# Attention and a mixture of experts on one core: the router steps' maximum moved, a second xT buffer, and late splits, one-hots and transposes placed later

## The chip, the cores and the metric

The kernel runs on one core of one Trainium2 chip. A core has a matrix engine (TensorE, PE in the profile; its weight loads are listed as PEld), a vector engine (VectorE, DVE), an activation engine (ScalarE, ACT), a general engine (GpSimd, POOL) and a queue that issues transfers (SyncE, SP). The engines run their own streams of instructions in order and wait for each other by semaphores. The metric is the device time of one execution in microseconds; lower is better.

## The reference

Attention over 8 batches, 8 heads, 576 positions and head size 64, with two masks: the first four heads see the last 32 positions ("local"), the other four see the positions with the same remainder modulo 32 ("strided"). The result, 4608 tokens of 512 numbers, goes through a mixture of 8 experts, each token through one of them at most.

```python
mask_local = (rel >= 0) & (rel < 32)
mask_strided = (rel >= 0) & (pos[None, :] % 32 == pos[:, None] % 32)
scores = np.where(masks[None], scale * q @ k.T, -1e9)      # heads 0-3 local, 4-7 strided
attn = exp(scores - max(scores)); attn /= attn.sum() + 1e-9
x = (attn @ v).transpose(0, 2, 1, 3).reshape(4608, 512)
skip_score = x @ w_skip; logits = x @ w_gate
e_idx = argmax(logits); gate_w = softmax(logits)[e_idx]
for e in range(8):
    h = maximum(x[mask_e] @ w1[e], 0)
    y[mask_e] = gate_w * (h @ w2[e])
out = x + y where skip_score > 0, else x
```

## The kernel before

Attention is cut into 32 units, four per batch: the local heads' blocks in two halves, `pr` 0 (blocks 0 to 4) and 1 (blocks 5 to 8), and the strided heads' in two halves, `pr` 2 and 3. The main loop (line 879) runs one step `n` for each unit and keeps a software pipeline: in step n it computes the scores of unit n+2 (`qk`), the exponentials of unit n (`tex`: transposes on PE, exponentials on ACT), the product with v of unit n-1 (`pv`) and the transposes of the output of unit n-2 (`xpose`, into the tile `xT`). All four are generators: each `next` issues one stage, so the loop writes the order of the engines' streams by hand.

`qk` has three stages: the score matmuls into the single PSUM buffer S (L211); the addition of the mask on DVE (L219 local, L221 strided), which frees S; the maximum on DVE (L225) with its subtraction on POOL (L227). `pv` has two: the matmuls into the single buffer PV (L281), and the normalization on DVE (L290, L291, L297), which frees PV. `tex` of the unit waits for POOL's subtraction (transposes at L247, exponentials at L255).

Each batch also has router work. `score` (L342; copied to `s64` by ACT at L349 and L351) multiplies the transposed outputs `xT` with the router's weights, at step `pr` 2 of the next batch; in that step the new batch's local outputs are transposed ahead of it on PE, and ACT copies them into `xT` (L327). At `pr` 3, the "router step", `route1` transposes the scores (L366) and makes the decision in a chain of ten small DVE operations (L371 to L389); one step on `route2` ranks the tokens (matmuls L416 to L422, DVE L429 to L433). Some steps later `gates` (L406 to L410) splits the gate values, `hot` makes one-hot tiles on DVE (`heh` L451, `hlo` L454), `mul` makes `hpm` on POOL (L462), and `place` (L470) multiplies them on PE into a table of tokens for each expert; the dictionary `plan` gives the step of each for each batch. At step 29 the table of batches 0 to 5 is finished (`tabled`, L481 to L486), and POOL gathers the rows of the first expert, key "e" (L639). Its weights come early: `FETCH` gives the steps at which their loads are issued on SP (L586, three buffers `raw`), `CASTS` those at which ACT makes the high part (L597), `RESTS` those at which DVE makes the low part (`wrest`, L603), which frees the raw buffer.

Router steps differ by batch. Up to batch 5 (`CB`) the router's DVE chain comes last in the step, and the maximum of that step's `qk` (the local second half of the next batch, 768 wide) is held (`held`) until the next step, behind that step's mask. From batch 6 on the whole router decision is run ahead of `tex` and of the mask.

On PE, DVE and POOL the order is that of the program; ACT and SP are ordered by the compiler's planner within the dependencies. After the loop (L995) PE transposes the gathered rows (`xrows`, L675, with the split of the result at L678 and L679), the expert's first product starts (`ffn1a`, L721), and the seven other experts follow, each as three matmuls for the split operands (L682 to L684).

Of the kernel before, what the change touches and what calls it, by code (L numbers as in the profile page):

```python
# [9 lines left out]
F32 = mybir.dt.float32  # L10
F32R = mybir.dt.float32r
BF16 = mybir.dt.bfloat16
# [7 lines left out]
B, H, S, D = 8, 8, 576, 64  # L20
# [6 lines left out]
SQ = 3 * NA  # L27
SB = 11
# [15 lines left out]
PB = 3  # L44
CB = 5
CASTS = [(6, 0), (6, 2)]
RESTS = [(6, 3), (7, 0)]
FETCH = [(6, 0), (6, 1), (6, 2), (7, 1)]
CE = (96, 3)

# [56 lines left out]
def attn_moe(ctx: ExitStack, tc: tile.TileContext, q, k, v, w9d, w1d, w2d, cst, out, NB=B):  # L107
# [22 lines left out]
    psum, bufs = pctx.enter_context(tc.tile_pool(name="psum", bufs=1, space=PSUM)), {"S": 1, "T": 4, "PV": 1}  # L130

    def ps(tag, n=1):
        return psum.tile([128, n, 512] if n > 1 else [128, 512], F32, name=tag, tag=tag, bufs=bufs[tag])
# [3 lines left out]
    ap = actx.enter_context(tc.tile_pool(name="apool", bufs=1))  # L137
# [26 lines left out]
    def passed(m):  # L164
        mark[:] = [m.ins]
# [14 lines left out]
    def loadq(b, kind):  # L180
        t, d = qtile(b, kind)
        for j in range(2):
            paced(t[:, j], d[:, j])
# [129 lines left out]
    xT_ = {}  # L313

    def xpose(b, pr):
        kind, b0, b1 = UNITS[pr]
        if b0 == 0:
            xT_[b, kind] = ap.tile([128, 2, (S, SB * SQ)[kind]], F32, name=f"xT{kind}", tag=f"xT{kind}", bufs=1)
        x, nq = xt_[b, kind], (HP, SQ)[kind]
        for g in range(b0, b1, 4):  # L320
            m = min(4, b1 - g)
            t = ps("T")
            for y in range(m):
                i = T.transpose(t[:, y * 128:(y + 1) * 128], x[:, g + y, :], ident)  # L324
            passed(i)
            yield
            A.copy(xT_[b, kind][:, :, g * nq:(g + m) * nq].rearrange("p i (n q) -> p n i q", q=nq),  # L327
                   t[:, 0:m * 128].rearrange("p (n i q) -> p n i q", i=2, q=HP)[:, :, :, 0:nq])
# [4 lines left out]
    def tiles(g):  # L333
        return GT
# [108 lines left out]
    def hot(g):  # L443
        o = slice(GOFF[g], GOFF[g + 1])

        def sp(n, shape, dt=F32, bufs=1):
            return ap.tile([128, GT] + shape, dt, name=n, tag=n, bufs=bufs)

        q, c = hot_[g]
        eh = sp("heh", [24], BF16)  # L450
        V.tensor_tensor(eh, con["eh"].unsqueeze(1).broadcast_to([128, GT, 24]),  # L451
                        c.unsqueeze(2).broadcast_to([128, GT, 24]), op=ALU.is_equal)
        lo = sp("hlo", [128], BF16, 2)
        V.tensor_tensor(lo, con["iom"].unsqueeze(1).broadcast_to([128, GT, 128]),  # L454
                        q.unsqueeze(2).broadcast_to([128, GT, 128]), op=ALU.is_equal)
        hot_[g] = lo, eh
# [364 lines left out]
    def weave(a, b):  # L821
        def chain(gs):
            for g in gs:
                yield from g
        a, b = chain(a), chain(b)
        live = [a, b]
        while live:
            for g in list(live):
                if next(g, 0) == 0:
                    live.remove(g)  # L830
# [9 lines left out]
    def run(*gs):  # L840
        weave(gs, [])
# [27 lines left out]
    mark.clear()  # L869
    fill = setup()  # L870
    tvw = table.rearrange("(e r) c -> e r c", e=NE)
    late, ranked, held = [], None, []

    plan = {x: (4 * x + 8, 4 * x + 10, 4 * x + 10, 4 * x + 12) for x in range(CB - 1)}
    plan[CB - 1] = (4 * CB + 4, 4 * CB + 5, 4 * CB + 5, 4 * CB + 7)
    plan[CB] = (4 * CB + 7, 4 * CB + 7, 4 * CB + 7, 4 * CB + 9)
    pool_order = ExitStack()
    pool_order.enter_context(tc.manual_schedule(engines={G.engine, T.engine, V.engine}))
    for n, (b, pr) in enumerate(units):

        ahead = n // 2 + 3
        qk_, v_, out_ = pr % 2 and ahead // 2 < NB, pr % 2 == 0 and b + 1 < NB, n > 3 and units[n - 4 + (pr + 1) % 2]
        if n == 8:
            spare = tvw[:, CMAX:CE[0] * CE[1] + CT, :].rearrange("e (a n) c -> a e (n c)", n=NE)
            nc.sync.dma_start(spare, fill.rearrange("p n c -> p (n c)")[0:spare.shape[0]].unsqueeze(1)
                              .broadcast_to([spare.shape[0], NE, 4 * NE]))
        if n + LA >= len(units) and "h" not in pool:
            zctx.close()
            pool["h"] = ctx.enter_context(tc.tile_pool(name="hpool", bufs=1, side="right", reuse_waits="tile"))
        g = [i for i, x in enumerate(GROUPS) if x[1] == b]  # L890

        front = [qk(*units[n + LA])] if n + LA < len(units) else []
        if n > 0:
            front.append(pv(*units[n - 1]))
        seq = [tex(b, pr)]
        if g and pr == 2:
            seq = [xpose(*units[n - 2])] + seq
        for x in front[:-1]:
            next(x)

        if late and b > CB:
            run(*late)
            late = []
            norm(g[0])
            ranked = g[0]
        if n > 0:
            run(seq.pop(0))
        if late:
            next(late[0])
        if qk_:  # L910
            loadq(ahead // 2, ahead % 2)
        if v_:
            loadv(b + 1, pr // 2, (0,))
        next(front[-1])
        if qk_:
            loadk(ahead // 2, ahead % 2)
        if v_:
            loadv(b + 1, pr // 2, (1,))
        put = [place(x) for x, it in plan.items() if it[3] == n]
        full = n == plan[CB][3]  # L920
        rank = []
        if ranked is not None:
            rank = [route2(ranked, of=COUNTED.get(b if pr else b - 1))]
            for _ in range(tiles(ranked) + 1):
                next(rank[0])
            ranked = None
        for x in front:
            next(x, 0)
            if held:
                run(*held)  # L930
                held = []
        if late:
            run(*rank, *late, *front[1:])
            held = front[:1]
        else:
            run(*rank, *front)
        if full:
            run(*put)
            tabled()
        late = []  # L940
        if b > 0 and pr == 2:
            seq = [score(b - 1)] + seq
        if n > 1 and not (g and pr == 2):
            seq.append(xpose(*units[n - 2]))
        run(*seq)
        if v_:
            loadv(b + 1, pr // 2, (2,))
        if out_:
            store(out_[0], out_[1] // 2, (pr % 2,))
        if not full:  # L950
            run(*put)
        if g and pr == 2:
            late = [route1(g[0])]
        if g and pr == 3 and b <= CB:
            norm(g[0])
            ranked = g[0]
        if b == PB + 2 and pr == 1:
            picked = pick(PB)
            next(picked)
        if b == PB + 2 and pr == 2:  # L960
            run(picked)
        if (b, pr) in RESTS:
            j = RESTS.index((b, pr))
            wrest("e", j, j + 1)
        if (b, pr) in CASTS:
            j = CASTS.index((b, pr))
            wcast("e", j, j + 1)
        if b == CB + 2 and pr == 3:
            count(CB)
        if n == 1:  # L970
            G.tensor_copy(parts[:, :, 0:2], con["pk"].rearrange("p (t c) -> p t c", c=2))
        for x, it in plan.items():
            for f, at in zip((gates, hot, mul), it):
                if at == n:
                    f(x)
        if b == PB + 2 and pr == 3:
            e0 = nc.sync.value_load(isel[0:1, 0:1], min_val=0, max_val=NE - 1)
            wdma("e", e0, 0, 1)
        if b == PB + 2 and pr == 3:
            s0 = G.value_load(isel[0:1, 0:1], min_val=0, max_val=NE - 1)  # L980
        if (b, pr) in FETCH:
            j = FETCH.index((b, pr)) + 1
            wdma("e", e0, j, j + 1)
        if b == CB + 2 and pr == 1:
            at, P = seat("e", *CE), CE[0]
            for c, dt in ((slice(0, 2), I32), (slice(2, 3), F32)):
                G.tensor_copy(at[:, :, c].bitcast(dt),
                              tabs[:P, bass.ds(s0, 1), 0:CE[1], c].rearrange("p o n c -> p (o n) c").bitcast(dt))
            gather("e", "e", "e", last=(CB + 1) * S)
# [16 lines left out]
    psum, bufs = pctx.enter_context(tc.tile_pool(name="psumT", bufs=1, space=PSUM, reuse_waits="tile")), {"S": 2, "T": 3, "PV": 2, "R": 1}  # L1006
# [24 lines left out]
    psum, bufs = ctx.enter_context(tc.tile_pool(name="psumB", bufs=1, space=PSUM, reuse_waits="tile")), {"S": 4, "T": 2, "PV": 2}  # L1031

    seq = [("e", e0, 6), ("e", e0, 7)]
# [176 lines left out]
```

## Time and profile before

| | |
|---|---|
| median of 3 runs | 441.22 us (441.03 to 444.55) |
| profiled execution | 442.9 us, its span 441.4 us |
| PE busy | 408.3 us (93%) |
| DVE busy | 274.9 us (62%) |
| ACT busy | 185.6 us (42%) |
| POOL busy | 144.8 us (33%) |
| mean granted clock of PE | 0.965 |
| moved by DMA | 90.39 MB |

The span runs from the first to the last instruction; the profiled execution's own time holds 1.5 us more around it. Attention takes the first 175 us, the experts the rest. A row of the timeline gives the start and the duration in us, the engine, the line, the operation, what it writes and reads, how often, and in brackets how long the engine was idle before it and what ended that. A row of the windows gives a stretch, its length, the busy time of PE, PEld, DVE, ACT and POOL with the number of instructions, the granted clock of PE, the DMA engines' busy share and GB/s. A row of the waits gives the waiting instruction, what released it, the total us, the count and the longest.

### The profile page before, as it was taken

The numbers are of one execution on the slowest core, as the hardware profiler recorded it, in microseconds if no ns is written. First come the engines' busy times: TensorE is split into PE (matmuls) and PEld (weight loads), VectorE is DVE, ScalarE is ACT, GpSimd is POOL, SyncE is SP. The second block draws the span as 40 slices with busy tenths as digits, with TensorE's granted clock in tenths as the row PEclk, the third lists the DMA queues.
The fourth block names the chain that finished last, engine by engine and source line by source line (L and its number), as shares of the span: only waits on it lengthen the run. The fifth ranks groups of instructions, "written<-read, shape, count | busy, mean of one in ns | idle before, by whom it ended". The sixth has DMA issues, their size and how long they took to land.

```text
span 441.4 us, 12232 instructions
## 1 busy us (share of the span) xinstructions
PE 408.3 (93%) x4991; PEld 367.1 (83%) x4992; DVE 274.9 (62%) x597; ACT 185.6 (42%) x361; POOL 144.8 (33%) x201
## 2 busy tenths in 40 slices
PE   5989899988988788998999999999999999999994
PEld 3867767767676668798898799999999999999984
DVE  3566879797997866760594564374564654855611
ACT  1345453644537244532642444453543544545400
POOL 3434445454644653214052236032023132201201
PEclk8899999999999685999999999999999999999998
DMA  8999999799989354535257467366475565645101
GB/s 294 398 343 293 307 317 320 249 331 304 311 250 351 107 157 110 168 98 138 97 190 211 130 215 225 127 192 196 140 235 154 191 198 184 212 148 189 47 21 43
DMA packets 51774, 90.39 MB, mean 205 GB/s; under 512 B 8091, under 2 KB 27931, under 8 KB 51713
## 3 DMA queue, kind: packets, MB, share of 16 engines
q1 hardware_dynamic: 45249, 79.19, 54.5%
q0 software_dynamic: 6464, 10.37, 8.2%
q8 instruction: 40, 0.66, 0.6%
q14 instruction: 21, 0.17, 0.1%
HBM read 75.16 MB, written 14.91 MB: 204 GB/s over the span
## 4 chain that ended last, share of the span: by engine, by line
PE 71%; DMA 9%; DVE 7%; ACT 6%; POOL 3%; issue 2%; SPq 1%; POOLq 0%; ACTq 0%; DVEq 0%
PE S L682 16%; PE S L684 16%; PE S L683 16%; PE PV L281 6%; DMA vt<-in_vp_dram 3%; PE T L324 3%; PE T L247 3%; PE S L211 3%; ACT s L351 2%; PE T L342 2%; PE PV L774 2%; DMA qt<-in_qp_dram 2%; DMA xg<-out_dram,tab 2%; PE T L661 1%; POOL sm L227 1%
## 5 line engine op out<-in xcount | busy, mean ns | idle before, releaser
L682 PE MATMUL S<-xh,w1h 128*128 128x342 f32 (+6 forms) x248 | 78.5, 316 | 0.0
L762 POOL DMA_INDIRECT out_dram<-ot,tab x25 | 28.0, 1119 | 152.7 <-DVE ot L760 142.9
L684 PE MATMUL S<-xh,w1l 128*128 128x342 f32 (+6 forms) x248 | 76.8, 310 | 0.0
L683 PE MATMUL S<-xl,w1h 128*128 128x342 f32 (+6 forms) x248 | 76.7, 309 | 0.0
L682 PE MATMUL S<-hh,w2h 128*128 128x288 f32 (+5 forms) x192 | 59.5, 310 | 0.7 <-DVE hl L695 0.7
L684 PE MATMUL S<-hh,w2l 128*128 128x288 f32 (+5 forms) x192 | 58.0, 302 | 0.0
L683 PE MATMUL S<-hl,w2h 128*128 128x288 f32 (+5 forms) x192 | 58.0, 302 | 0.0
L694 ACT ACTIVATE hh<-S 128x342 fp32r<-128x342 f32 (+6 forms) x64 | 27.9, 436 | 64.1 <-PE S L684 55.9
L603 DVE TENSOR_TENSOR w1l<-raw,w1h 128x1024 fp32r<-128x1024 f32 x32 | 39.0, 1223 | 18.6 <-ACT w1h L597 17.8
L682 PEld LDWEIGHTS S<-xh,w1h 128*128 128x128 f32 x248 | 46.9, 189 | 0.7 <-DVE hl L695 0.5
L683 PEld LDWEIGHTS S<-xl,w1h 128*128 128x128 f32 x248 | 46.8, 189 | 0.1
L684 PEld LDWEIGHTS S<-xh,w1l 128*128 128x128 f32 x248 | 46.7, 188 | 0.0
L603 DVE TENSOR_TENSOR w2l<-raw,w2h 128x1024 fp32r<-128x1024 f32 x32 | 39.1, 1223 | 9.8 <-ACT w2h L597 9.6
L327 ACT COPY xT<-T 128x512 f32<-128x512 f32 (+4 forms) x56 | 22.2, 441 | 53.6 <-PE T L324 30.1
L227 POOL TENSOR_TENSOR sm<-sm,mx 128x480 f32<-128x480 f32 (+1 forms) x32 | 32.2, 1026 | 37.9 <-DVE mx L225 26.6
L639 POOL DMA_INDIRECT xg<-out_dram,tab x25 | 33.1, 1323 | 32.7 <-issue 10.1
L695 DVE SCALAR_TENSOR_TENSOR hl<-S,hh 128x342 fp32r<-128x342 f32 (+6 forms) x64 | 30.9, 483 | 20.2 <-ACT hh L694 18.8
L211 PE MATMUL S<-kt,qt 64*64 64x54 f32 (+1 forms) x1280 | 32.7, 243 | 8.2 <-DMA kt<-in_kp_dram 3.3
L211 PEld LDWEIGHTS S<-kt,qt 64*64 64x64 f32 x1280 | 27.0, 142 | 14.5 <-DVE sm L219 3.5
L682 PEld LDWEIGHTS S<-hh,w2h 128*128 128x128 f32 x192 | 36.2, 188 | 1.0 <-DVE hl L695 1.0
L683 PEld LDWEIGHTS S<-hl,w2h 128*128 128x128 f32 x192 | 36.3, 189 | 0.0
L684 PEld LDWEIGHTS S<-hh,w2l 128*128 128x128 f32 x192 | 36.2, 189 | 0.0
(182 smaller groups left out, 792.9 us busy)
## 6 DMA issues: line engine op xcount, KB each, us to landing
raw<-in_w_dram SPq DMA_DIRECT2D x64, 512.0 KB
vt<-in_vp_dram SPq DMA_DIRECT2D x40, 390.0 KB
qt<-in_qp_dram SPq DMA_DIRECT2D x16, 304.0 KB
kt<-in_kp_dram SPq DMA_DIRECT2D x16, 297.0 KB
out_dram<-x SPq DMA_DIRECT2D x16, 288.0 KB
kt<-in_kp_dram SPq DMA_DIRECT2D x14, 304.0 KB
qt<-in_qp_dram SPq DMA_DIRECT2D x14, 288.0 KB
out_dram<-x SPq DMA_DIRECT2D x32, 99.0 KB
```

Of the source, the lines that this page charges most:

```text
L211: m = T.matmul(s[HP * (i ^ j):HP * (i ^ j) + HP, j, (blk - b0) * win:(blk - b0 + 1) * win], lhsT=qt[p, j, blk * nq:blk * nq + HP], rhs=kt[ ...
L227: G.tensor_tensor(e[:, j], e[:, j], mx[:, j].unsqueeze(2).broadcast_to([128, b1 - b0, win]), op=ALU.subtract)
L281: x = T.matmul(p[HP * i:HP * i + HP, bank, slot * 65:slot * 65 + 65], lhsT=pt[a:z, m, j, i ^ j, :], rhs=vt[a:z, (b0 if kind == 0 else b0 / ...
L327: A.copy(xT_[b, kind][:, :, g * nq:(g + m) * nq].rearrange("p i (n q) -> p n i q", q=nq), t[:, 0:m * 128].rearrange("p (n i q) -> p n i q" ...
L603: V.tensor_tensor(lo, raw_.pop((key, j)), hi.bitcast(F32), op=ALU.subtract)
L639: i = G.indirect_dma_start(out=xg[:s["P"], t, :], out_offset=None, in_=out[0:last, :], in_offset=bass.IndirectOffsetOnAxis(ap=s["tab"][:s[ ...
L682: T.matmul(p, lhsT=a[0], rhs=b[0], start=start, stop=False)
L683: T.matmul(p, lhsT=a[0], rhs=b[1], start=False, stop=False)
L684: T.matmul(p, lhsT=a[1], rhs=b[0], start=False, stop=stop)
L694: A.activation(s["hh"][:, f, :C], p[:, :C], AF.Relu)
L695: V.scalar_tensor_tensor(s["hl"][:, f, :C], p[:, :C], 0.0, s["hh"][:, f, :C].bitcast(F32), op0=ALU.max, op1=ALU.subtract)
L762: i = G.indirect_dma_start(out=out, in_=ot[:P], in_offset=None, bounds_check=NTOK - 1, oob_is_err=False, out_offset=bass.IndirectOffsetOnA ...
```

## The change

Five things move. The local `xT` has two buffers instead of one, the strided one still has one; `hlo` has one instead of two. At the router steps up to batch 5 the maximum (and POOL's subtraction) comes right behind its mask, ahead of the normalization and of the router's DVE chain; nothing is held. At batch 6's router step the mask comes first, then `tex`, then the router's decision with its transposes, then the normalization, the ranks and the maximum; at batch 7's, which has no `qk`, `tex` comes ahead of the router's decision. `hot` and `mul` of batch 5 come at step 28 instead of 27. The low parts of the first two weight tiles (`RESTS`) come at steps 29 and 30 instead of 27 and 28.

```diff
-RESTS = [(6, 3), (7, 0)]
+RESTS = [(7, 1), (7, 2)]
...
-            xT_[b, kind] = ap.tile([128, 2, (S, SB * SQ)[kind]], F32, name=f"xT{kind}", tag=f"xT{kind}", bufs=1)
+            xT_[b, kind] = ap.tile([128, 2, (S, SB * SQ)[kind]], F32, name=f"xT{kind}", tag=f"xT{kind}", bufs=2 - kind)
...
-        lo = sp("hlo", [128], BF16, 2)
+        lo = sp("hlo", [128], BF16)
...
-    late, ranked, held = [], None, []
+    late, ranked = [], None
...
-    plan[CB] = (4 * CB + 7, 4 * CB + 7, 4 * CB + 7, 4 * CB + 9)
+    plan[CB] = (4 * CB + 7, 4 * CB + 8, 4 * CB + 8, 4 * CB + 9)
...
+        masked = late and b > CB and len(front) > 1
+        if masked:
+            next(front[0])
+        if n > 0:
+            run(seq.pop(0))
         if late and b > CB:
             run(*late)
             late = []
             norm(g[0])
             ranked = g[0]
-        if n > 0:
-            run(seq.pop(0))
...
-        for x in front:
+        for x in front[1:] if masked else front:
             next(x, 0)
-            if held:
-                run(*held)
-                held = []
-        if late:
-            run(*rank, *late, *front[1:])
-            held = front[:1]
-        else:
-            run(*rank, *front)
+            if late:
+                run(x)
+        run(*rank, *late, *front)
```

## The prediction

> **What bounds the kernel now.** The page's busy times come first, then the waits of TensorE in the attention steps, then the busy times of one batch.
>
> ```profile
> PE 408.3 (93%) x4991; PEld 367.1 (83%) x4992; DVE 274.9 (62%) x597; ACT 185.6 (42%) x361; POOL 144.8 (33%) x201
> ```
> ```profile
> PE T L247 <- POOL sm L227: 4.5, 8, 0.8
> PE T L247 <- ACT s L351: 1.7, 5, 0.3
> ...
> PE T L366 <- ACT pts L255: 1.1, 5, 0.2
> ```
> ```profile
> 116.77:135.57 18.80, 16.87 (x414) 13.34 (x409) 17.72 (x50) 8.90 (x22) 11.66 (x18) 1.00 0.87 283
> 135.57:159.62 24.05, 18.62 (x359) 14.79 (x350) 18.70 (x52) 11.11 (x23) 12.16 (x20) 0.86 0.60 192
> ```
>
> TensorE (PE) is busy 93% of the span, so whatever ends its waits is gain. The waits table covers 38 to 130 us: 4.5 us on GpSimd's subtraction of the maximum, 1.7 + 1.1 us behind ScalarE's copies of the scores. The last two rows (PE, weight loads, DVE, ACT, POOL, clock, DMA share, GB/s) are one batch of steps each, about the 6th and the 7th: the later one takes 5.2 us more and shows a clock of 0.86. VectorE (DVE) is the next engine: 17.7 of 18.8 us.
>
> **Part 1, the maximum behind its mask, steps 7 to 23.** At these router steps the maximum of the local second half is held until the next step.
>
> ```profile
> 98.55 0.96 DVE L219 TENSOR_TENSOR sm<-S,cs 128x768 f32<-128x768 f32 x1
> 101.43 0.17 DVE L290 TENSOR_SCALAR rc<-PV 128x12 f32<-128x12 f32 x1 [1.92 <-PE PV L281]
> ...
> 105.63 0.94 DVE L225 TENSOR_REDUCE mx<-sm 128x8 f32<-128x768 f32 x1
> ...
> 120.23 0.17 DVE L290 TENSOR_SCALAR rc<-PV 128x12 f32<-128x12 f32 x1
> ...
> 129.52 0.17 DVE L290 TENSOR_SCALAR rc<-PV 128x10 f32<-128x10 f32 x1 [0.26 <-PE PV L281]
> ```
> ```profile
> 106.72 1.61 POOL L227 TENSOR_TENSOR sm<-sm,mx 128x384 f32<-128x384 f32 x2 [1.56 <-DVE rc L290]
> ...
> 128.53 1.42 POOL L227 TENSOR_TENSOR frame<-frame,mx 128x324 f32<-128x324 f32 x2 [1.40 <-DVE mx L225]
> ```
>
> The mask ends at 99.51 and DVE then sits idle for 1.92 us. The 0.94 us maximum fits there (99.51 + 0.94 = 100.45, before 101.43), and the subtraction ends about 5 us earlier, so the 4.5 us of waits go. Queued behind the inserted maximum are the normalization and the router's DVE chain; while the slot is idle nobody waits. It is not idle at the fifth such step: between 101.43 and 129.52 DVE never pauses, and at 120.23 its normalization started right after the mask, so there it comes 0.86 us later.
>
> **Part 2, two xT buffers.**
>
> ```profile
> 115.33 0.75 ACT L327 COPY xT<-T 128x512 f32<-128x512 f32 x2 [3.36 <-PE T L342]
> ```
>
> ACT stands idle 3.36 us until the score matmuls have read the single buffer, then copies for 0.75 us ahead of the score copies. With a second buffer the copy falls into the idle time, the score copies start some 0.7 us earlier, and the 0.34 + 0.22 us waits of L247 and L366 (1.7 + 1.1 over five batches) go.
>
> ```profile
> PE T L247 <- POOL sm L227: 2.1, 4, 0.8
> ```
>
> This row is the same wait from 38 to 100 us only. Sum of both parts up to step 26: 4 x 0.56 + 2.1 = 4.4 by 101 us. In the stretch where DVE never pauses 3.0 us of waits are removed, but DVE is relieved by one maximum (0.86) only; followed through its order, the gain of PE at 130 us is 1.7, the S buffer and the PV buffer being free in time. **Term 1: 6.1 us.** Bounds: 7.3 if DVE did not matter, 0 if transfers take over.
>
> **Part 3, steps 27 to 30.** Here the long stall of the trace lies.
>
> ```profile
> 136.93 0.50 PE L366 MATMUL T<-cs,s 41*128 41x41 f32 x5 [0.90 <-ACT s L351]
> ...
> 148.03 1.33 PE L211 MATMUL S<-kt,qt 64*64 64x54 f32 x40 [3.04 <-DVE frame L221]
> ...
> 151.17 2.44 PE L281 MATMUL PV<-vt,ptl 96*64 96x65 f32 x40
> ```
> ```profile
> 109.29 1.39 PE L281 MATMUL PV<-vt,ptl 96*64 96x65 f32 x40
> ```
> ```profile
> 137.46 0.25 DVE L371 TENSOR_REDUCE s<-T 128x45 f32<-128x90 f32 x1 [1.83 <-PE T L366]
> ...
> 140.44 0.15 DVE L290 TENSOR_SCALAR rc<-PV 128x12 f32<-128x12 f32 x1
> ...
> 141.83 0.20 DVE L429 SCALAR_TENSOR_TENSOR T<-T,rohb 128x40 f32<-128x40 f32 x1
> ...
> 142.78 0.94 DVE L225 TENSOR_REDUCE mx<-sm 128x8 f32<-128x768 f32 x1
> ...
> 143.83 1.22 DVE L603 TENSOR_TENSOR w1l<-raw,w1h 128x1024 fp32r<-128x1024 f32 x1
> ...
> 145.06 0.81 DVE L451 TENSOR_TENSOR heh<-cs,hc 128x120 bf16<-128x120 f32 x1
> 145.79 1.44 DVE L454 TENSOR_TENSOR hlo<-cs,hq 128x640 bf16<-128x640 f32 x1
> ```
> ```profile
> 143.87 2.68 POOL L227 TENSOR_TENSOR sm<-sm,mx 128x384 f32<-128x384 f32 x2 [3.92 <-DVE mx L225]
> ...
> 148.20 1.19 POOL L462 TENSOR_TENSOR hpm<-heh,parts 128x600 bf16<-128x600 bf16 x1
> ```
>
> At 145 to 148 us PE waits 3.04 us for the mask at L221, because DVE first makes a split (1.22), then the one-hots (heh and hlo, 145.06 to 147.2). The change puts the split two steps later, the one-hots behind that mask, and lets step 27's mask fill the 1.83 us in which DVE waited for L366. So on PE go 3.04, 0.90 and two waits of some 0.3: 4.6 us. I follow DVE in the new order with the start-to-start times above: router chain 2.1 (137.46 to the mask at 139.57; the rank matmuls wait for most of it, of which the PV matmuls cover 1.0, so PE waits about 0.75), normalization 1.4, rank 0.95, maximum 0.9, then the mask at once; its S buffer is ready in time, so the 3.04 does not come back. What is late next is the place matmul L470 of step 29, which needs hlo (DVE) and hpm (POOL). Counted from the end of the maximum of step 27: DVE needs 0.3 for two small operations, 0.8 for the mask, 1.3 and 0.8 for normalization and the next maximum (3.1 so far), 1.0 for the one-hots. POOL subtracts (1.6), does four gate operations (1.0), waits for the maximum at 3.1, subtracts the frame (1.42; up to 2.3 beside the one-hots, as the 2.68 against 1.61 shows) and makes hpm (1.19): 5.7 to 6.6. PE passes L211 (0.8) at about 2.2, L247 (1.1) at 3.2 and the PV matmuls (1.39) at 4.5, so L470 waits 1.2 to 2.1 us; I take 1.7. Then the clock:
>
> ```profile
> 123.58:126.99 3.41, 2.37 (x62) 1.90 (x58) 3.29 (x11) 1.16 (x4) 1.77 (x4) 1.00 0.76 207
> ```
> ```profile
> 144.06:147.47 3.41, 0.94 (x12) 0.64 (x6) 3.41 (x5) 0.76 (x2) 3.33 (x4) 1.00 0.35 102
> 147.47:150.89 3.42, 2.86 (x48) 2.61 (x48) 3.35 (x9) 0.47 (x1) 2.42 (x5) 0.50 0.78 231
> 150.89:154.30 3.41, 3.41 (x49) 3.01 (x48) 1.49 (x5) 0.71 (x2) 1.55 (x2) 0.50 0.02 5
> ...
> 157.71:161.13 3.42, 1.54 (x17) 0.77 (x9) 1.11 (x5) 2.88 (x7) 1.86 (x4) 1.00 0.85 239
> ```
>
> After the stretch with 0.94 us of PE work the granted clock is 0.50 for 6.8 us. The 40 PV matmuls take 2.44 us in it and 1.39 at full clock, so the 6.27 us of work there would take 3.6: price 2.7 us. The same follows the stretch with 1.54, not the one with 2.37 of 3.41. **Term 2:** 4.6 + 2.7 - 0.75 - 1.7 = 4.8, say **4.6 us** with hlo slowed beside POOL; bounds 2 (the half clock stays) and 7.3 (no new wait).
>
> **Part 4, step 30 to the first FFN matmuls.**
>
> ```profile
> 156.89 1.18 PE L342 MATMUL T<-xT,w 128*32 128x288 f32 x16
> ...
> 160.96 0.67 PE L366 MATMUL T<-cs,s 41*128 41x41 f32 x5 [1.73 <-ACT s L351]
> ...
> 165.70 0.85 PE L675 MATMUL T<-cs,xg 96*128 96x96 f32 x4
> ...
> 171.96 0.61 PE L721 MATMUL S<-xh,w1h 128*128 128x288 f32 x1 [1.16 <-DVE xl L679]
> ```
>
> From L342 to L721 lie 15.1 us, 10.8 of them at half clock (161.13 to 171.96). In the new order, tex of step 31 ahead of the router's transposes and the score copies 0.7 earlier, the 1.73 us wait shrinks to about 0.5; behind that DVE's chain (router, normalization, rank, splits of the gathered rows) carries the end, and I add 12.9 us: **term 3, 2.2 us**. The eight L721 before 174.78 run at half clock; at full clock **term 4, 1.2 us**. The two moved splits (2 x 1.22 on DVE) land behind steps 29 and 30, before L371 of step 31, in time DVE has: L371 follows L366, so DVE too stands through the 1.73 us in which PE waits for ACT. Without that cover they cost up to 2.4.
>
> Everything after is PE work at 93% and more, on a chain that starts from these matmuls, so it shifts as a whole. 6.1 + 4.6 + 2.2 + 1.2 = 14.1 us if the clock never halves. The 1.2 to 2.1 us wait at L470 leaves 38 to 65% of a 3.41 us stretch busy, between 45% (halved) and 69% (not); with it the waits at steps 27 and 31. I take one halved stretch, -2.7: **11.4 us.** The profiled execution took 442.9 (span 441.4 and 1.5 around it), which gives 431.5; the median 441.2 is 1.7 lower, so **430 us**.
>
> **The rivals.**
>
> *The clock never halves:* 14.1 us, 427. For it: three of the four waits that halved it are gone. Against it: the 1.54 row, whose longest wait is 1.73 us. The Trainium skill, "TensorE: Matmul & The Clock Gate", HAM oscillation, has the clock halve only after idle gaps above some 3.4 us; by that rule nothing halves and the time is this rival's. The trace disagrees: the waits before its two halvings are 3.04 and 1.73 us.
>
> *Transfers take over:* the DMA share is 0.87 to 0.98 in these batches, and term 1 asks for 7% more per us. For it: that share. Against it: no row of the waits between 38 and 130 us names a load. Term 1 falls to near 0: 436.
>
> *SP keeps its order:* the split frees the raw buffer for the fourth weight load.
>
> ```profile
> 145.07 0.39 SPq L586 DMA_DIRECT2D raw<-in_w_dram  x1
> ```
> ```profile
> 159.28 1.22 POOL L639 DMA_INDIRECT xg<-out_dram,tab  x1 [1.09 <-DMA out_dram<-x]
> ```
> ```profile
> xg<-out_dram,tab POOLq DMA_INDIRECT x25, 3.6
> ```
>
> In before it issues at 145.07, right at the split's end (143.83 + 1.22), with the last stores of batch 5 behind it on SP. If it still stands ahead of them, they wait until step 29's split, and the gather of rows behind them. In before the gather issues 6.4 us ahead of its first use (L675, 165.70). The split (1.22), the issue of the raw load and three stores (0.4 each) and their landing would push it back by some 5 to 7 us; from issue to landing a gather takes 3.6 (last column of the last row, a median), so some 2.8 are to spare: cost about 3, 433. SP's order is the planner's, which may pass a load that waits.
>
> *The other side, slower:* PE at half clock all the way. The change makes PE wait for DVE and POOL in many short pieces (0.75, 1.7, 0.5, 0.75). If each 3.41 us stretch from step 27 to L721 falls under the bound of 45 to 69%, some 30 us of steps with 25 us of PE work run at 2.44/1.39 = 1.76 times; that is up to 19 us, 14.1 - 19 = -5, and overlap with DVE waits gives back a part: 443 to 446. It decides only when the waits reach 1.1 us or more in each stretch.
>
> *It does not do what it says:* the planner lays ACT or SP so that the waits stay: 441.
>
> **How the numbers follow.** One halved stretch (430) 0.40, none (427) 0.25, transfers (436) 0.12, SP's order (433) 0.12, half clock throughout (443 to 446) 0.05, no effect 0.06. The range 425 to 437 holds the first four, with an edge for 7.3 in term 1. A measurement tells about 1% (4.4 us) from no change: faster 0.85, within 1% 0.11, slower 0.04.
>
> **What would show it.** Right: no wait of L247 on POOL's sm and of L366 on ACT in steps 11 to 25; no 3 us wait at L211 in step 28; a wait of 1 to 2 us before L470 of step 29; score to score 17 to 18.8 us. Wrong: waits of PE on kt or qt loads, stores of batch 5 issued after the fourth raw load, several half-clock stretches before L721, or a gain at L721 that the gathers behind it give back.

## The result, and the profile after

| | before | after |
|---|---|---|
| median (16 runs each) | 441.56 us (437.73 to 446.58) | 436.38 us (431.27 to 439.61) |
| ratio, with its 95% interval | | 0.9875 (0.9842 to 0.9908) |
| profiled execution, its span | 442.9, 441.4 us | 436.3, 434.7 us |
| mean granted clock in it | 0.965 | 0.975 |

The ratio leaves out the executions more than 1.5% above the fastest of their kernel, 4 of the 16 after. It is 5.5 us (4.1 to 7.0), just under half of the 11.4 forecast. The busy times of the kernel after, and the granted clock in 40 slices of its span:

```profile
PE 403.2 (93%) x4991; PEld 364.5 (84%) x4992; DVE 274.0 (63%) x597; ACT 186.2 (43%) x361; POOL 143.1 (33%) x201
...
PEclk9799999999999958999999999999999999999999
```

PE's share is again 93%: the waits went, and so did 5 us of PE time, but not its idle share. The waits of PE from 37 to 124 us, the stretch that answers to 38 to 130 us of before (total us, count, longest):

```profile
PE S L211 <- issue: 1.4, 2, 0.8
PE PV L281 <- issue: 1.1, 1, 1.1
PE T L366 <- ACT pts L255: 1.1, 5, 0.2
PE T L416 <- DVE rohb L386: 0.7, 1, 0.7
PE T L247 <- ACT s L351: 0.3, 2, 0.2
```

The 4.5 us of L247 behind POOL are gone and 1.4 of its 1.7 behind ACT; L366's 1.1 us stand as before. PE in steps 27 to 31 (start, duration, idle time before it):

```profile
131.58 0.50 PE L366 MATMUL T<-cs,s 41*128 41x41 f32 x5 [0.22 <-ACT pts L255]
...
134.24 0.19 PE L416 MATMUL T<-rohb,tri 128*128 128x40 bf16 x1 [1.24 <-DVE rohb L386]
...
139.06 0.80 PE L211 MATMUL S<-kt,qt 64*64 64x54 f32 x40
...
144.31 0.42 PE L470 MATMUL T<-hpm,hlo 128*128 128x120 bf16 x5 [2.12 <-POOL hpm L462]
...
147.13 1.18 PE L342 MATMUL T<-xT,w 128*32 128x288 f32 x16
...
150.62 0.40 PE L247 MATMUL T<-cs,frame 128*54 128x128 f32 x2 [1.08 <-ACT s L351]
151.24 0.50 PE L366 MATMUL T<-cs,s 41*128 41x41 f32 x5 [0.22 <-ACT pts L255]
...
153.45 0.22 PE L416 MATMUL T<-rohb,tri 128*128 128x40 bf16 x1 [0.80 <-DVE rohb L386]
...
158.20 0.87 PE L675 MATMUL T<-cs,xg 96*128 96x96 f32 x4 [3.43 <-DMA xg<-out_dram,tab]
```

The 3.04 us at L211 are gone. In their place stand 1.24 (the router's chain on DVE), 2.12 (hpm) and a new 3.43 us: the gathered rows come late. At L342 of step 30, PE was 9.8 us ahead of before (156.89 to 147.13); at L721 (171.96 to 163.89) only 8.1. DVE, SP and POOL, each from its own timeline, show why:

```profile
146.63 1.22 DVE L603 TENSOR_TENSOR w1l<-raw,w1h 128x1024 fp32r<-128x1024 f32 x1
```
```profile
130.86 5.05 SPq L160 DMA_DIRECT2D out_dram<-x  x5
147.88 0.39 SPq L586 DMA_DIRECT2D raw<-in_w_dram  x1
148.31 1.74 SPq L160 DMA_DIRECT2D out_dram<-x  x3
```
```profile
146.80 1.23 POOL L985 COPY tab<-tabs 96x6 int32 x2 [1.09 <-DVE tabs L486]
152.90 1.22 POOL L639 DMA_INDIRECT xg<-out_dram,tab  x1 [4.87 <-issue]
```

The split moved to step 29 ends at 147.85; at 147.88 SP issues the fourth weight load, which waited for that split's buffer; the first of the three stores behind it is batch 5's last. The landing records of the trace have it landed by about 152, and POOL, done with its table at 148.03, gathers at 152.90. The profile names no releaser for these 4.87 us ("issue"); that it is the store is read from this order on SP, and fetch_late below tests it. Five stores had left in time from 130.86 on; the planner set the raw load between the second and the third of the last three.

The clock, in 3.41 us stretches (PE, PEld, DVE, ACT, POOL, clock, DMA share, GB/s):

```profile
149.74:153.16 3.42, 1.81 (x55) 1.36 (x55) 1.56 (x7) 2.65 (x7) 0.26 (x1) 1.00 1.01 306
153.16:156.57 3.41, 1.32 (x11) 0.92 (x11) 3.03 (x16) 0.58 (x1) 2.81 (x3) 0.50 0.91 274
156.57:159.98 3.41, 1.79 (x38) 1.59 (x40) 0.88 (x5) 0.48 (x1) 0.98 (x5) 0.50 0.71 232
159.98:163.40 3.41, 3.34 (x30) 2.92 (x24) 2.01 (x8) 1.28 (x4) 0.00 (x0) 0.50 0.01 2
163.40:166.81 3.41, 2.92 (x12) 2.91 (x13) 2.69 (x5) 2.33 (x3) 2.07 (x3) 0.50 0.73 165
```

The clock is halved for 13.65 us, against 20.5 in the profile before (6.83 from 147.47, 13.65 from 161.13).

### The profile page after: what moved, and what is told of

Read it like the earlier page. It is cut to its first block, busy times and chain, and to the rows that moved or that the text cites. A ratio compares the mean times of both kernels' runs of the same rounds, so it can differ in the third digit from the quotient of the medians.

```text
span 434.7 us, 12244 instructions
## 1 busy us (share of the span) xinstructions
PE 403.2 (93%) x4991; PEld 364.5 (84%) x4992; DVE 274.0 (63%) x597; ACT 186.2 (43%) x361; POOL 143.1 (33%) x201
## 4 chain that ended last, share of the span: by engine, by line
PE 70%; DMA 9%; DVE 9%; ACT 4%; issue 4%; SPq 1%; POOL 1%; POOLq 0%; ACTq 0%; DVEq 0%
PE S L682 16%; PE S L684 16%; PE S L683 16%; PE PV L281 5%; DMA vt<-in_vp_dram 3%; PE T L324 3%; PE S L211 3%; DMA xg<-out_dram,tab 3%; PE T L247 3%; ACT s L351 2%; PE PV L774 2%; PE T L661 2%; DMA kt<-in_kp_dram 1%; DVE x L297 1%; PE T L342 1%
## 5 line engine op out<-in xcount | busy, mean ns | idle before, releaser
L682 PE MATMUL S<-xh,w1h 128*128 128x342 f32 (+6 forms) x248 | 78.4, 316 | 0.0
L682 PE MATMUL S<-hh,w2h 128*128 128x288 f32 (+5 forms) x192 | 59.4, 310 | 0.8 <-DVE hl L695 0.8
L682 PEld LDWEIGHTS S<-xh,w1h 128*128 128x128 f32 x248 | 46.9, 189 | 0.7 <-DVE hl L695 0.5
L227 POOL TENSOR_TENSOR sm<-sm,mx 128x480 f32<-128x480 f32 (+1 forms) x32 | 30.7, 980 | 29.2 <-DVE mx L225 20.6
L211 PE MATMUL S<-kt,qt 64*64 64x54 f32 (+1 forms) x1280 | 32.9, 243 | 6.9 <-DMA kt<-in_kp_dram 4.2
L211 PEld LDWEIGHTS S<-kt,qt 64*64 64x64 f32 x1280 | 27.2, 141 | 13.6 <-issue 4.3
L327 ACT COPY xT<-T 128x512 f32<-128x512 f32 (+4 forms) x56 | 22.1, 442 | 36.5 <-PE T L324 36.5
L682 PEld LDWEIGHTS S<-hh,w2h 128*128 128x128 f32 x192 | 36.1, 188 | 1.0 <-DVE hl L695 1.0
```

What stands on the lines that cost most here:

```text
L211: m = T.matmul(s[HP * (i ^ j):HP * (i ^ j) + HP, j, (blk - b0) * win:(blk - b0 + 1) * win], lhsT=qt[p, j, blk * nq:blk * nq + HP], rhs=kt[ ...
L227: G.tensor_tensor(e[:, j], e[:, j], mx[:, j].unsqueeze(2).broadcast_to([128, b1 - b0, win]), op=ALU.subtract)
L682: T.matmul(p, lhsT=a[0], rhs=b[0], start=start, stop=False)
```

## The experiments

Theory: three things hold back the gain, the blocked gather, new waits in place of the old ones, and a clock that the change does not mend. Rivals: transfers take over; the early parts share their gain; the late part is worth nothing by itself.

The clock differs between executions of one kernel, so it has to be taken out of small differences. In the 80 executions of the kernel before that enter these ratios (438.2 to 446.7 us, mean clocks 0.962 to 0.988, five chips) an execution took 2.1 us less for each 0.01 more on the same chip (correlation -0.82). The last column is the mean time carried to a clock of 0.975 with this slope; it was reckoned after the runs. Two limits go with it. An edit can change the clock by changing the waits, and the column then takes out that part of its worth too. And by the spread of the executions, a difference of two rows is good to about 1.5 us only, to 0.8 for two rows of twelve (an estimate: twice the standard error). Means and clocks are of the executions that enter the ratio. Medians, ratios and intervals are as measured, each against the kernel before on the same chip.

| kernel | median us | ratio (interval) | mean us | mean clock | at 0.975 |
|---|---|---|---|---|---|
| before | 441.98 | | 442.1 | 0.9753 | 442.2 |
| after | 436.38 | 0.9875 (0.9842-0.9908) | 435.6 | 0.9747 | 435.6 |
| fetch_late | 432.83 | 0.9811 (0.9765-0.9856) | 432.4 | 0.9769 | 432.8 |
| fetch_alone | 441.59 | 0.9958 (0.9924-0.9991) | 441.4 | 0.9785 | 442.2 |
| splits_early | 435.66 | 0.9858 (0.9806-0.991) | 435.4 | 0.9750 | 435.4 |
| max_alone | 436.43 | 0.9876 (0.9834-0.9919) | 435.7 | 0.9809 | 437.0 |
| xt_alone | 436.92 | 0.9904 (0.9867-0.994) | 437.6 | 0.9793 | 438.5 |
| max_xt | 436.5 | 0.9855 (0.9802-0.9909) | 436.6 | 0.9708 | 435.7 |
| late_alone | 442.76 | 1.0006 (0.9975-1.0036) | 443.0 | 0.9702 | 442.0 |
| late_fetch | 439.32 | 0.9907 (0.9872-0.9942) | 439.3 | 0.9762 | 439.6 |
| max_xt_fetch | 436.47 | 0.9888 (0.9841-0.9935) | 436.4 | 0.9732 | 436.0 |
| splits_only | 431.78 | 0.9757 (0.9719-0.9794) | 431.7 | 0.9785 | 432.4 |
| hots_early | 431.89 | 0.98 (0.9753-0.9847) | 432.4 | 0.9785 | 433.2 |
| router_first | 431.19 | 0.9784 (0.974-0.9829) | 431.4 | 0.9862 | 433.8 |
| before_warm | 437.61 | 0.9886 (0.9854-0.9919) | 437.6 | 0.9893 | 440.7 |
| after_warm | 432.59 | 0.9798 (0.9748-0.9847) | 433.2 | 0.9867 | 435.7 |
| fetch_warm | 430.83 | 0.9772 (0.9719-0.9824) | 431.0 | 0.9858 | 433.2 |
| hots_warm | 431.89 | 0.9756 (0.9712-0.9801) | 431.6 | 0.9820 | 433.1 |
| splits_warm | 434.62 | 0.9824 (0.9777-0.9872) | 434.5 | 0.9770 | 434.9 |

### The blocked gather: fetch_late, fetch_alone, splits_early

fetch_late is the changed kernel, fetch_alone the kernel before, both with this edit:

```diff
-FETCH = [(6, 0), (6, 1), (6, 2), (7, 1)]
+FETCH = [(6, 0), (6, 1), (7, 1), (7, 2)]
```

> The changed kernel with the loads of the fourth and fifth weight tile issued at steps 29 and 30 (behind the splits that free their buffers) instead of 26 and 29. Theory: in the changed kernel the 4th raw load waits on SP for step 29's split with a store of batch 5 behind it, and this alone holds the gather (POOL 4.87 us idle, L675 3.43 us late). Then the gather issues near 149 us, right behind POOL's copy of the table (146.80 + 1.23 and about 1.1), its first part lands by about 153, L675 at 154.8 waits for nothing, L721 comes about 3 us sooner (near 161), and the time is 3 us lower than the changed kernel's: about 433, ratio to before about 0.981. Rival: the gather is slow because transfers share the queues there (a landing 5 us behind the issue), and L675 still waits 1.5 to 3 us: ratio 0.986 to 0.988. Second rival: the later weight tiles now come late, a new wait of PE for w1 behind L721 takes the gain back: L721 at 161, ratio 0.986 to 0.99.

> The kernel before with nothing changed but the loads of the fourth and fifth weight tile, issued at steps 29 and 30: a control for the run that moved them in the changed kernel. Theory: there they held the gather, here they hold nothing (the gather issues 6.4 us ahead of its use), so no change: 441, ratio 0.998 to 1.002. Rival: it was not the order but the transfers, 0.5 MB less beside the stores and the gather, that made the difference: 2 to 4 us faster here too, ratio 0.991 to 0.995. Second rival: the tiles come late for the matmuls at L682: 1 to 2 us slower, ratio 1.003.

POOL's and PE's timelines of fetch_late:

```profile
146.01 1.23 POOL L985 COPY tab<-tabs 96x6 int32 x2 [0.87 <-DVE tabs L486]
147.41 1.22 POOL L639 DMA_INDIRECT xg<-out_dram,tab  x1 [0.17 <-POOL tab L985]
```
```profile
153.31 0.49 PE L675 MATMUL T<-cs,xg 96*128 96x96 f32 x4
...
158.71 0.37 PE L721 MATMUL S<-xh,w1h 128*128 128x288 f32 x1 [1.32 <-DVE xl L679]
```

The gather now issues 0.17 us behind its table instead of 4.87, L675 waits for nothing, and L721 comes at 158.71 instead of 163.89 (here the clock halved once between 17 and 426 us, for 3.41 us). The ratio is the expected one. The control moved too: its 0.9958 lies between the 0.998 to 1.002 that were expected and the 0.991 to 0.995 of the rival. But its executions had the higher clock, and at 0.975 it stands where before stands. Taken as measured, without the clock, the control would leave 1.0 of the 2.8 us between after and fetch_late to the blocked gather (0.9811/0.9958 is 0.985). That the moved load itself changes the clock was not tested.

splits_early is the changed kernel with the splits as before:

```diff
-RESTS = [(7, 1), (7, 2)]
+RESTS = [(6, 3), (7, 0)]
```

> The changed kernel with the two low parts of the weight tiles back at steps 27 and 28. Theory: each split costs its 1.22 us on DVE ahead of a mask or the one-hots, and the raw load goes out at once, so the gather's wait goes. L211 of step 28 or 29 waits about 1 us, L470 of step 29 waits about 3.3 instead of 2.12, L675's 3.43 is gone: up to 1 us lower than the changed kernel, 435 to 436, ratio 0.985 to 0.988. Rival: the moved splits carried the gain of the stall at 145 us, so L211 waits 2 to 3 us again and the clock halves twice before L675: 438 to 440, ratio 0.992 to 0.997.

```profile
141.08 0.80 PE L211 MATMUL S<-kt,qt 64*64 64x54 f32 x40 [0.91 <-DVE frame L221]
...
147.31 0.66 PE L470 MATMUL T<-hpm,hlo 128*128 128x120 bf16 x5 [3.10 <-POOL hpm L462]
...
159.54 0.49 PE L675 MATMUL T<-cs,xg 96*128 96x96 f32 x4
```

As the theory had it, 0.91 at L211, 3.10 at L470 and nothing at L675: the time is even with the changed kernel. So moving the splits bought 1.9 us of waits and paid for it with a blocked gather.

### The early parts: max_alone, xt_alone, max_xt

Each is the kernel before with one part, or with both.

```diff
-        if late:
-            run(*rank, *late, *front[1:])
-            held = front[:1]
-        else:
-            run(*rank, *front)
+            if late:
+                run(x)
+        run(*rank, *late, *front)
```
```diff
-... tag=f"xT{kind}", bufs=1)
+... tag=f"xT{kind}", bufs=2 - kind)
-        lo = sp("hlo", [128], BF16, 2)
+        lo = sp("hlo", [128], BF16)
```

> The kernel before with only the maximum right behind its mask at the router steps up to batch 5; xT has one buffer, steps 27 to 31 as before. Theory (the prediction's split of its first term): 2.1 us by 101 us and about 3 us at L366 of step 27 (136.9 to 133.9); from there all shifts, 438.5, ratio 0.993. Rival 1: the maximum carries nearly all of the 5.64 us that the changed kernel gains there, because its waits of L366 behind ACT remained: 3 us by 101 us, 4.3 at step 27, ratio 0.990. Rival 2: the stall at step 28 waits for DVE, which does not come sooner, and takes the gain back: 3 to 4 us at step 27, under 1.5 at L721, ratio 0.997 to 1.0.

> The kernel before with only the two buffers of xT (and one of hlo). Theory (the prediction's split): 0.56 us per batch, L366 at 99.97 moves to about 97.7 and that of step 27 by 2.8 us; time 438.5 to 439, ratio 0.994. Rival: it takes 0.2 to 0.35 us per batch only, as the waits of L366 for ACT of 0.22 us still stand in the changed kernel's trace: 0.8 to 1.4 us by 101 us, 1.0 to 1.7 at step 27, ratio 0.996 to 1.0.

> The kernel before with both early parts, the maximum right behind its mask and two buffers of xT; steps 27 to 31 as before. Theory: the two parts add up, as the medians of each alone do (441.0 to 436.4 is 4.6 us, to 436.9 is 4.1): 8.7 us, 432.3, ratio 0.980. Then steps 27 to 31 of the whole change bring nothing but the blocked gather. Rival: they share their waits, and the 5.3 to 5.6 us that the changed kernel has gained at step 27 is all there is: 435.5, ratio 0.987 to 0.988; then the late part is worth what the gather takes away.

PE's waits from 38 to 125 us, first of max_alone, then of xt_alone, then of max_xt:

```profile
PE T L247 <- ACT s L351: 1.7, 5, 0.4
PE T L366 <- ACT pts L255: 1.1, 5, 0.2
```
```profile
PE T L247 <- POOL sm L227: 5.1, 8, 1.0
PE T L366 <- ACT pts L255: 1.1, 5, 0.2
PE T L247 <- ACT s L351: 0.5, 3, 0.2
```
```profile
PE T L366 <- ACT pts L255: 1.1, 5, 0.2
PE T L247 <- ACT s L351: 0.3, 2, 0.2
```

Both parts alone came out below the lowest ratio that was expected of them (0.990 and 0.994), though not clear of their intervals. The maximum removes all eight waits behind POOL, 4.5 us, also in the stretch where DVE never pauses. The second buffer removes 1.2 of L247's 1.7 and none of L366's, whose releaser is the exponential (pts, L255) and not the copy of the scores. Later waits shrink a little with it (L366 of step 31 from 1.73 to 1.49). xt_alone's 3.7 us at equal clock are more than these waits add up to; where the rest comes from stays open. Both together gain 6.5 at equal clock, less than 5.2 + 3.7, and the ratio lies by the rival's. The profiles show it otherwise: the scores of step 26, at 132.86 in before, come 4.0 us sooner in max_alone (128.88), 0.8 in xt_alone (132.10) and 6.3 in max_xt (126.52), which is more than the sum. So the size of both together is shown, but not that the parts share it.

### The late part: late_alone, late_fetch, max_xt_fetch

late_alone is the changed kernel without the early parts, late_fetch the same with the later loads, max_xt_fetch is max_xt with them.

> The changed kernel with one buffer of xT and with the maximum held until the next step as before: only steps 27 to 31 of the change are left. Theory (the prediction's terms 2 to 4 with one halved stretch, less the gather's 3.4): 4.6 + 2.2 + 1.2 - 2.7 - 3.4 is 1.9 us, 439.1, ratio 0.996. L675 waits about 3.4 us again. Rival: the late part is worth nothing beside the blocked gather (the stall of 3.04 us at step 28 comes back as waits at L470 and L416): 3.4 us slower, 444.4, ratio 1.008.

> The same, with the loads of the fourth and fifth weight tile issued at steps 29 and 30: the late part without the blocked gather. Theory: 5.3 us, 435.7, ratio 0.988; L675 waits for nothing. Rival (the late part is worth nothing by itself): 441, ratio 0.998 to 1.002.

> The kernel before with the maximum behind its mask, two buffers of xT and the later loads of the fourth and fifth weight tile; of the late part (splits, one-hots, router transposes at steps 27 to 31) nothing. Compared with the changed kernel with the later loads (ratio 0.981) it gives what the late part is worth when no gather is blocked. Theory: the late part is worth the 2 to 3 us by which it lay below its control without the early parts (0.9907 against 0.9958): ratio 0.986. Rival: it is worth nothing beside the early parts, the ratios multiply (0.9855 x 0.9958): 0.981.

late_fetch (0.9907) came out nearer to its theory (0.988) than to its rival (0.998 to 1.002), max_xt_fetch (0.9888) above both of its own (0.986 and 0.981). With the gather blocked the late part is worth nothing: 1.0006, between the 0.996 and 1.008 that were expected, and after (0.9875) lies by max_xt (0.9855). Without the block it is worth 2.6 us (442.2 to 439.6) or 3.2 (436.0 to 432.8), at equal clock. The block costs 2.4 (442.0 to 439.6) or 2.8 (435.6 to 432.8).

### Which edit of the late part: hots_early, router_first, splits_only

The first two are fetch_late with one edit undone; splits_only is max_xt_fetch with the splits at steps 29 and 30, that is, fetch_late with both undone.

```diff
-    plan[CB] = (4 * CB + 7, 4 * CB + 8, 4 * CB + 8, 4 * CB + 9)
+    plan[CB] = (4 * CB + 7, 4 * CB + 7, 4 * CB + 7, 4 * CB + 9)
```
```diff
-        masked = late and b > CB and len(front) > 1
-        if masked:
-            next(front[0])
-        if n > 0:
-            run(seq.pop(0))
         if late and b > CB:
...
+        if n > 0:
+            run(seq.pop(0))
```

> The changed kernel with the later loads, and with the one-hots and hpm of batch 5 back at step 27. Theory: heh and hlo (2.2 us on DVE) stand ahead of the mask of step 28 again, so L211 of that step waits about 2 us; the 1.73 us wait of L470 goes, as hpm is ready sooner: even, ratio 0.980 to 0.983. Rival: L470 waits for POOL's subtractions ahead of hpm and not for the one-hots, so its wait stays at 1 us or more and the 2 us at L211 come on top: 1.5 to 2 us more, ratio 0.985.

> The changed kernel with the later loads, and with the router's decision of batches 6 and 7 ahead of the transposes and the mask again, as before the change. Theory: the waits of L366 for ACT's copy of the scores return (0.9 and 1.7 us), and those of L416 for DVE's router chain (1.24 and 0.82) and of L247 (1.08) go, so the reorder only renamed the wait: within 0.7 us, ratio 0.980 to 0.983. Rival (the prediction's third term): the reorder is worth 2 us or more: ratio 0.986.

> The kernel before with both early parts, later loads, and of the late part only the low parts of the weight tiles two steps later (the one-hots at step 27 and the router's decision first, as before). Theory: the splits carry the worth of the late part: L211 of step 28 waits 1.8 us instead of 3.03 (the split's 1.22 less), and the time is that of the changed kernel with later loads, ratio 0.980 to 0.982. Rival: the 2.2 us of one-hots ahead of the mask still halve the clock and the worth comes only with their move or the router's: 0.985 to 0.989.

PE in hots_early, in router_first and in splits_only:

```profile
141.67 0.44 PE L470 MATMUL T<-hpm,hlo 128*128 128x120 bf16 x5
```
```profile
143.23 0.42 PE L470 MATMUL T<-hpm,hlo 128*128 128x120 bf16 x5 [2.12 <-POOL hpm L462]
149.54 0.50 PE L366 MATMUL T<-cs,s 41*128 41x41 f32 x5 [1.51 <-ACT s L351]
151.91 0.19 PE L416 MATMUL T<-rohb,tri 128*128 128x40 bf16 x1
```
```profile
139.72 0.80 PE L211 MATMUL S<-kt,qt 64*64 64x54 f32 x40 [1.34 <-DVE frame L221]
...
142.78 0.44 PE L470 MATMUL T<-hpm,hlo 128*128 128x120 bf16 x5
```

The splits alone carry the late part (436.0 to 432.4 at equal clock), with 1.34 us at L211 where 1.8 was expected. With early one-hots no wait is left at L470, and the 2 us expected at L211 did not come either. With the router first the 1.51 at L366 return and the 0.82 at L416 and 1.08 at L247 go: the wait has another name. The move of the one-hots is worth 0.4 us and that of the router 1.0 at equal clock, inside the intervals, and by the ratios as measured both moves cost something (0.980 and 0.9784 without them, 0.9811 with them); so neither a gain nor a cost of them is shown.

### The clock: before_warm, after_warm, fetch_warm, hots_warm, splits_warm

Each puts matmuls of zeros on PE in front of the instruction that waits, into a PSUM tile that the next matmul overwrites; the order of the rest stays.

```diff
+    def warm(n, p):
+        for _ in range(n):
+            T.matmul(p.rearrange("p (a b) -> p a b", b=128), lhsT=dummy,
+                     rhs=dummy.unsqueeze(1).broadcast_to([128, 4, 128]), start=True, stop=True)
...
         sc = ps(tag)
+        warm({5: 3, 6: 6}.get(g, 0), sc)
...
+        if n == 28:
+            warm(11, ps("T"))
```

This is before_warm; the others name their places in their expectations (fetch_warm's names steps 23 and 30 for rank matmuls; steps 24 and 31 are meant). The added lines move the numbers behind them: L414 here is the zeros, and L675 becomes L685 in after_warm and L682 in splits_warm.

> The kernel before with 20 matmuls of zeros on PE in its waits: three ahead of L366 of step 27 (0.90 us), eleven ahead of L211 of step 28 (3.04 us) and six ahead of L366 of step 31 (1.73 us). No order is changed. Theory: the half clock comes from these waits; the mean granted clock of the executions rises from 0.975 (0.972 to 0.977 by chip) to 0.983 or more and the time falls by 2 to 3 us, ratio 0.994: this is what the prediction took the change to win by its clock. Rival: the halvings have other causes, clock 0.975, ratio 1.0 or up to 1.003 for zeros that end late.

> The changed kernel with the gather blocked as it is, and matmuls of zeros in its waits: two, four and three ahead of the rank matmuls of steps 24, 27 and 31, six ahead of the place matmul of step 29 (2.12 us), twelve ahead of the transposes of the gathered rows (3.43 us). Theory: clock from 0.973 to 0.983 or more, 2 to 3 us less than the changed kernel, ratio 0.981; the 3.4 us of the blocked gather still stand between this and the run with later loads and zeros (0.977). Rival: clock and time as in the changed kernel, 0.9875.

> The changed kernel with the later loads, and 15 matmuls of zeros (128x128 by 128x512, bf16) put on PE where it waits: two, four and three ahead of the rank matmuls of steps 23, 27 and 30 (waits of 0.67, 1.24, 0.82 us) and six ahead of the place matmul of step 29 (1.73 us). They write a PSUM tile that the next matmul overwrites. Theory: the stretches of half clock behind 120 us come from these short waits, and their number differs from one execution to the next because the 3.41 us stretches lie differently: the mean granted clock of the executions rises from 0.977 to 0.983 or more, and the time falls by about 2 us, ratio 0.976. Rival: the halvings come from other places (the start, the transposes of the gathered rows, L721): mean clock 0.977, time as without the zeros or up to 1 us more, ratio 0.981 to 0.984.

> The changed kernel with later loads, the one-hots at step 27 (which left no wait at L470 and none at L211), and matmuls of zeros ahead of the rank matmuls of steps 24, 27 and 31. Theory: waits and half clock both gone: mean clock 0.985 or more, 429 us, ratio 0.973. Rival: the other waits (0.61 at L324, 1.07 at L247, those of the gathered rows) still halve it: clock 0.979, ratio 0.979.

> The kernel before with both early parts, later loads and later splits (the run at 0.976), and 16 matmuls of zeros on PE: two ahead of the rank matmuls of step 24 (0.68 us), three ahead of L366 of step 27 (0.72), five ahead of L211 of step 28 (1.34) and six ahead of L366 of step 31 (1.52). Theory: the clock adds to the order: mean clock from 0.978 to 0.986 or more, 2 us less: 429.5, ratio 0.970. Rival: as with the zeros in the changed kernel with later loads, the halvings behind the gathered rows remain and nothing is left to gain: clock 0.980, ratio 0.975.

The clock of before_warm in 40 slices, and L211 of step 28, whose remaining wait follows the zeros:

```profile
PEclk9899899999999999999999999999999999999999
```
```profile
149.66 0.80 PE L211 MATMUL S<-kt,qt 64*64 64x54 f32 x40 [1.63 <-DVE frame L221]
```

Twenty matmuls of zeros in the kernel before, with nothing moved, raise the mean clock of its executions from 0.974 to 0.989 and win 1.1% (0.8 to 1.5), where 0.6% was expected: nearly as much as the whole change. By the slope above, the clock accounts for 3.2 of these 4.9 us. In the changed kernel they raise it from 0.975 (0.973 over all 16 executions) to 0.987 and the ratio falls to 0.980. In after_warm the zeros fill part of the wait for the rows:

```profile
153.78 2.75 PE L414 MATMUL T<-dummy 128*128 128x512 bf16 x12
158.34 0.55 PE L685 MATMUL T<-cs,xg 96*128 96x96 f32 x4 [1.81 <-DMA xg<-out_dram,tab]
```

and the block shows a third time: 435.7 against 433.2 of fetch_warm. splits_warm missed both its expectations: clock 0.977, and slower than splits_only. Its gather issued at 150.20 instead of 148.53 and landed late:

```profile
PE T L682 <- DMA xg<-out_dram,tab: 3.1, 2, 1.9
```

Of the 1.7 us, 1.4 were there before any zeros: L211 comes at 84.72 instead of 83.30. Why the rows then landed so late is not settled. fetch_warm did as the theory had it (432.8 to 430.8 us, clock 0.986), hots_warm by half (0.982, 0.976). The best two are splits_only and hots_warm, both at 0.976; both beat the changed kernel.

The profiles of before_warm and after_warm have no halved stretch between 53 and 427 us, so they compare the late steps at full clock: the scores (L342) of steps 26 and 30, and the expert's first product (L721, here L727 and L731):

```profile
134.46 1.18 PE L342 MATMUL T<-xT,w 128*32 128x288 f32 x16
...
156.57 1.18 PE L342 MATMUL T<-xT,w 128*32 128x288 f32 x16
...
168.77 0.40 PE L727 MATMUL S<-xh,w1h 128*128 128x288 f32 x1 [0.57 <-ACT xh L684]
```
```profile
127.36 1.18 PE L342 MATMUL T<-xT,w 128*32 128x288 f32 x16
...
146.79 1.18 PE L342 MATMUL T<-xT,w 128*32 128x288 f32 x16
...
161.94 0.40 PE L731 MATMUL S<-xh,w1h 128*128 128x288 f32 x1 [0.74 <-ACT xh L688]
```

From step 26 to step 30 the old order takes 22.1 us and the new one 19.4: here the late part wins 2.7. From step 30 to the first product it is 12.2 against 15.2, with the gather blocked in the second. Without the block the new order takes 12.4 (fetch_late, 146.31 to 158.71) and the old router order in it 12.2 (router_first, 146.05 to 158.20), also at full clock. So in this last stretch the late part wins nothing, and the block costs about 3 us.

## Why the prediction was wrong

The range held the time; the size did not. By its steps:

- **Term 1** (6.1 for the early parts) was right: max_xt gives 6.5 at equal clock, and 6.3 at the scores of step 26, so the rival of the transfers, with this term near 0, did not come true. Its parts were not: 4.5 us of the waits are the maximum's, also where the prediction let DVE hold back 1.3 of the 3.0 us, and L366's 1.1 us were put down to the xT copy, though the quoted row named pts as releaser.
- **"SP keeps its order"**, a rival at 0.12 that the sum left at nothing, came true, at its named place and nearly at its price: some 3 was said, L675 waited 3.43, and the runs give 2.4 to 2.8. This is the step whose failure cost most. The sentence that weighed it ("the planner's, which may pass a load that waits") had no row behind it; the trace of before already showed stores of batch 5 behind that load.
- **Term 2** was right in this pair of profiles: 9.76 - 5.35 = 4.4 us from L366 of step 27 to L342 of step 30, against 4.6. Without its 2.7 of clock it was 1.9; at full clock the new order takes 2.7 us less from the scores of step 26 to those of step 30 (22.1 to 19.4). New waits were nearly as forecast: 1.24 (0.75) and 2.12 (1.7, bounds 1.2 to 2.1).
- **Term 3** (2.2) failed: the 1.73 us wait was to shrink to 0.5; it became 1.08 + 0.22 and 0.80. L342 to L721 took 16.8 us, not 12.9; without the block and at full clock it takes 12.4, so the 12.9 was nearly right. What was wrong is the 15.1 that it was compared with: 10.8 of them were at half clock, and at full clock the old order takes 12.2 (before_warm). So the 2.2 us were clock, not order. Without the block, terms 2 and 3 should have given 4.1 us besides the clock (4.6 - 2.7 + 2.2); 2.6 to 3.2 were measured.
- **The clock terms** (2.7 gone, 1.2 more, 2.7 lost again: 1.2 net) failed in their basis. The profiled execution had a clock of 0.965; the 80 executions average 0.975, and the changed kernel's no more (0.975; 0.973 over all 16). One execution's 20.5 us of half clock was taken for the kernel's.

So 6.1 + 4.1 + 1.2 was forecast; 6.5 + about 3 - about 2.6 + 0 was found, near the 6.6 of the whole change at equal clock. The further 1.1 us to the measured 5.5 lies inside the interval. That the time fell inside the range is owed to its upper edge, 437, which was set for the rivals (transfers 436, SP's order 433), and not to the sum. Three of the four marks of being wrong that the prediction had set for itself are in the profile after: stores of batch 5 behind the fourth raw load (as in before already), several half-clock stretches before L721 (from 153.16 on), and a gain that is given back (of the 8.1 us at L721, 6.9 are left at 215 us, as the next gathers come late).

In the kernel before, the **half clock** is shown to follow its short waits: filling them removes it there (before_warm). In splits_warm, at 0.977, the longest halving of the profile (10.24 us from 157.16) follows the first wait for the rows (1.20 us), which no zeros filled. The halving at 153.16 in the profile after follows a stretch in which PE was busy for 1.81 of 3.42 us and no wait was longer than 1.08 (L247). The prediction's bound, halved at 45% and not at 69%, holds for it, but not for all runs: in fetch_alone a stretch with PE busy for 1.57 of 3.41 us (46%, from 146.15) was not followed by a halving, and in fetch_warm one with 2.40 of 3.41 (70%, from 148.85) was. The Trainium skill, "TensorE: Matmul & The Clock Gate", HAM oscillation, asks for idle gaps above some 3.4 us, which this contradicts; its section "A second HAM failure mode: psum-queue depth-cycling" has frequent short idling throttle the clock too, and with that before_warm agrees.

## What to carry to other kernels

When a step is moved, write down the queue behind every instruction that its buffers release: here a DVE split moved by two steps held a weight load, the load a store, the store a gather, the gather PE. Judge changes of 1% by many executions and their clocks, and never price a half-clock stretch from one profile; before a new order is credited with time, compare both orders at the same clock. Where PE must wait a microsecond, cheap filler can be worth as much as a reordering (before_warm), but it has to be measured each time (splits_warm).

## What was not expected of the hardware

The mean granted clock of one program, the kernel before, ran from 0.962 to 0.988 between executions, by the slope 5.5 us. Halved stretches lasted 3.41, 6.83, 10.24 or 13.65 us, multiples of one period, apart from the last one of each run, which the end cuts off. In fetch_late the stretch ahead of a halving (132.87 to 136.29) holds no wait longer than 1.24 us, while another run (router_first, waits of 2.12 and 1.51) shows no halved stretch between 16.4 and 426 us; what decides between them is open, and neither the longest wait nor PE's busy share of a stretch alone tells it.
